# A longer-annealed instruction order for a sliding-window attention and gated convolution kernel

## The chip, the core and the metric

The kernel runs on one core of one Trainium2 chip. The metric is the device time of one execution in microseconds; a lower number is better. The core has five engines that run at the same time, each through its own list of instructions in order: TensorE (PE, with its weight loads shown apart as PEld), VectorE (DVE), ScalarE (ACT), GpSimd (POOL), and SyncE (SP), which here only issues DMA transfers. They meet at semaphores.

## The reference

Attention over 8 batches and 8 heads, 576 positions and head size 64, in which a position sees only the 32 positions on either side, followed by a feed-forward block with a three-tap convolution along the sequence and a sigmoid gate:

```python
# attention: q, k, v are (8, 8, 576, 64)
scores = scale * np.matmul(q, k.transpose(0, 1, 3, 2))
mask = np.abs(pos[:, None] - pos[None, :]) <= 32
scores = np.where(mask, scores, -1000000000.0)
attn = softmax(scores)
x = np.matmul(attn, v)            # heads put side by side: (8, 576, 512)
# feed-forward block
h = np.maximum(x @ w_in, 0.0)     # 512 -> 1024
conv_out[s] = sum(conv_w[k] * h[s + k - 1] for k in range(3))   # per channel, zeros outside
out = h * sigmoid(conv_out) @ w_out                              # 1024 -> 512
```

All inputs and the output are 32-bit floats.

## The kernel before

**The work.** The attention is done batch by batch, and each batch in two halves of 288 rows (`attention(b)`, s = 0 and 1). A half is loaded by SP into staging tiles (`load_qk`, `load_v`), cast to bf16 (`cast_qk` into qn and kn, `cast_v` and `shift_v` into ve and vo; for batches after the second these casts are POOL's alone), transposed on PE and copied to qT and kT (`transposes`), multiplied into 128 x 64 score blocks (`scores`: L669), put through the exponential on ACT (L684), multiplied with v (`values`: L712), normalised on DVE (L730, L732) and transposed into xT (`turn`: on PE for the first two batches, by a DMA transpose of SP for the others).

The feed-forward block works on 12 chunks of 384 rows, three for each pair of batches. `hidden` makes eight tiles of 128 channels for a chunk: four matmuls with w_in (L857), a relu with a factor of one half on ACT (L877) into hT, the three taps, a tanh on ACT (L955, since sigmoid(x) is half of one plus tanh(x/2)), and the gate on DVE (L972) into gT. `project` multiplies gT with w_out (L997), copies the result to y (on ACT or DVE), and SP stores y (L1015, for the last chunk L1011). Two large weight matrices are loaded through two staging tiles wst and cast (`load_w`).

**The choices.** Some operations can be done in several ways, and the number in `CHOICE` says how.

- For each group of scores, 0 adds the mask's large negative number on PE ahead of the scores (L658, with the constant tile `band`), 1 multiplies the exponentials by a 0/1 mask on POOL, 2 does so on DVE (both are L691).
- For the taps of each of the eight tiles of a chunk, the list `KINDS` says which taps are done on PE (L932, with a diagonal weight matrix), on ACT (L940), on DVE (L945) and on POOL (L920 for the product, L925 for the sum): 0 is two taps on PE and one on DVE, 1 is one on PE and two on DVE, 2 is one on ACT and two on DVE, 3 is all three on POOL (three instructions and then two more), 4 is all three on PE.

**The order.** Nothing in the kernel is scheduled by the compiler. `Plan.add` records every operation with what it reads and writes. `Plan.place` then walks through the operations as the list `ORDER` names them, takes the engine from `PICK` where an operation may run on more than one (casts, copies, diagonal weights, y), takes a PSUM bank from `BANKS` for each operation that opens a PSUM slot (there are eight banks), and gives each operation a planned start. The instructions are emitted in the order of the planned starts. So the four lists CHOICE, ORDER, PICK and BANKS decide every engine's list of instructions, and which operations share a bank. `WARM` adds matmuls that compute nothing into gaps of the first 36 planned microseconds (L1024); there are 19 of them.

**Names that the text uses.** "A tap" on ACT is L940, on DVE L945; "a mask" is L691; a "POOL pair" is the three instructions L920, L920, L925 and a "POOL single" the two L920, L925 that follow it for choice 3. tmp is the tile in which POOL gathers its taps; the tanh that follows reads it. Lines of the changed kernel are smaller by one.

```python
        if alt is not None:
            if CHOICE[alt[0]] not in alt[1]:
                return None
...
        order, banks = [self.ops[i] for i in ORDER], iter(BANKS)
        for op in order:
            e = op.eng = PICK.get(op.idx) or next(iter(op.on))
```

Of the kernel before, what the change touches and what calls it, by code (L numbers as in the profile page):

```python
# [17 lines left out]
    0, 0, 2, 0, 0, 2, 0, 2, 2, 0, 4, 4, 4, 3, 4, 4, 4, 4, 0, 4, 0, 4, 4, 4, 0, 4, 2, 2, 0, 0, 1, 4,  # L18
    0, 4, 0, 4, 0, 4, 4, 4, 0, 0, 4, 2, 4, 0, 2, 2, 2, 2, 0, 2, 2, 4, 0, 3, 2, 4, 4, 2, 2, 4, 3, 3,
    2, 2, 2, 2, 2, 0, 0, 1, 2, 2, 3, 2, 1, 1, 4, 2, 2, 2, 0, 2, 2, 2, 4, 2, 3, 0, 2, 4, 3, 2, 2, 3,  # L20
    2, 1, 2, 2, 3, 2, 2, 0, 0, 2, 2, 2, 2, 1, 4, 3, 2, 4, 3, 0, 2, 0, 2, 2, 1, 2, 0, 2, 3, 2, 3, 2,
    0, 2, 2, 3, 2, 2, 3, 2, 3, 2, 2, 2, 3, 1, 3, 2, 2, 3, 2, 0, 2, 2, 3, 3,
# [11 lines left out]
    30, 37, 0, 1, 2, 11, 9, 29, 36, 51, 47, 28, 52, 35, 27, 34, 45, 46, 49, 50, 48, 55, 56, 53, 31,  # L34
    18, 38, 41, 26, 68, 75, 32, 42, 43, 33, 44, 24, 3, 39, 60, 17, 20, 16, 61, 7, 6, 54, 57, 70, 77,
    69, 76, 91, 87, 88, 67, 74, 85, 86, 89, 58, 59, 62, 92, 63, 64, 65, 90, 22, 117, 121, 120, 4,
    98, 96, 97, 99, 66, 225, 227, 226, 15, 228, 10, 118, 112, 113, 40, 73, 93, 94, 25, 8, 213, 71,
    81, 115, 251, 214, 80, 135, 142, 217, 221, 222, 119, 242, 218, 252, 235, 223, 84, 13, 5, 243,
    114, 215, 224, 236, 14, 95, 116, 219, 220, 23, 72, 82, 253, 79, 83, 244, 237, 78, 103, 104, 105,
    134, 141, 154, 100, 150, 21, 155, 133, 140, 132, 139, 152, 148, 248, 216, 153, 101, 102, 110,  # L40
    149, 111, 106, 108, 109, 238, 151, 159, 239, 249, 107, 254, 266, 232, 268, 160, 250, 256, 267,
    290, 386, 229, 19, 255, 269, 291, 136, 174, 137, 138, 146, 257, 233, 230, 387, 234, 264, 376,
    265, 156, 377, 292, 231, 12, 293, 258, 382, 245, 262, 259, 157, 263, 383, 274, 384, 385, 260,
    261, 240, 275, 277, 380, 246, 284, 158, 180, 278, 241, 279, 381, 281, 388, 389, 247, 280, 171,
    172, 306, 143, 144, 177, 178, 147, 390, 294, 276, 285, 286, 282, 270, 295, 283, 391, 185, 186,
    164, 271, 173, 179, 191, 192, 413, 287, 272, 296, 414, 165, 166, 161, 406, 307, 312, 145, 305,
    304, 311, 162, 392, 273, 163, 393, 394, 288, 289, 187, 378, 189, 169, 416, 379, 188, 167, 409,
    170, 168, 419, 415, 410, 190, 417, 407, 408, 418, 420, 199, 200, 320, 321, 193, 122, 126, 124,
    125, 123, 395, 324, 322, 411, 402, 412, 435, 127, 323, 399, 194, 436, 403, 437, 400, 404, 401,
    325, 396, 195, 397, 421, 398, 318, 319, 422, 129, 131, 128, 130, 297, 298, 196, 326, 329, 438,  # L50
    197, 330, 308, 313, 176, 182, 175, 183, 184, 405, 439, 198, 466, 467, 331, 181, 201, 202, 204,
    203, 205, 301, 340, 341, 346, 356, 343, 342, 347, 354, 327, 440, 206, 441, 309, 316, 328, 357,
    423, 431, 358, 352, 353, 302, 355, 432, 359, 424, 427, 425, 426, 428, 310, 317, 314, 332, 333,
    334, 364, 365, 362, 363, 335, 336, 337, 315, 360, 361, 474, 473, 480, 491, 492, 433, 434, 207,
    457, 442, 449, 429, 446, 299, 461, 458, 443, 450, 462, 451, 463, 444, 459, 460, 447, 448, 430,
    208, 445, 366, 209, 211, 487, 345, 344, 475, 476, 350, 348, 511, 510, 509, 481, 454, 493, 351,
    452, 464, 210, 212, 453, 455, 494, 489, 490, 552, 553, 300, 465, 349, 367, 456, 488, 370, 371,
    372, 368, 369, 498, 499, 515, 525, 500, 526, 546, 547, 495, 496, 554, 555, 512, 516, 521, 522,
    523, 524, 660, 661, 667, 678, 497, 679, 527, 528, 548, 549, 550, 529, 674, 551, 530, 570, 562,
    571, 675, 572, 532, 534, 535, 533, 563, 573, 531, 578, 468, 469, 574, 479, 478, 486, 483, 477,  # L60
    482, 485, 504, 505, 501, 502, 506, 558, 559, 560, 567, 503, 579, 536, 561, 589, 580, 575, 576,
    577, 581, 582, 513, 519, 339, 374, 373, 568, 338, 603, 605, 601, 606, 602, 564, 484, 514, 520,
    470, 586, 565, 604, 471, 590, 569, 566, 591, 592, 587, 518, 517, 540, 541, 542, 537, 538, 588,
    593, 609, 610, 556, 617, 611, 607, 557, 583, 612, 539, 613, 633, 625, 626, 608, 627, 697, 618,
    634, 622, 614, 584, 662, 695, 698, 702, 663, 508, 375, 507, 732, 733, 635, 619, 628, 585, 623,
    624, 668, 734, 735, 709, 710, 638, 676, 736, 620, 621, 639, 636, 637, 737, 680, 792, 629, 696,
    701, 303, 793, 799, 596, 681, 643, 677, 597, 644, 645, 707, 708, 711, 712, 640, 594, 595, 646,
    738, 806, 807, 630, 631, 632, 647, 641, 642, 713, 714, 739, 615, 616, 748, 749, 598, 720, 715,
    648, 649, 810, 599, 700, 794, 795, 753, 721, 716, 717, 718, 650, 651, 750, 811, 652, 740, 741,
    722, 685, 682, 683, 800, 686, 746, 747, 757, 665, 664, 672, 704, 670, 699, 703, 706, 669, 666,  # L70
    673, 762, 744, 763, 767, 764, 765, 768, 769, 545, 544, 543, 869, 870, 770, 751, 758, 766, 745,
    754, 759, 752, 684, 472, 653, 657, 654, 771, 755, 760, 761, 808, 775, 809, 658, 655, 656, 780,
    719, 705, 889, 671, 796, 690, 812, 813, 865, 866, 742, 875, 797, 827, 828, 983, 829, 801, 833,
    881, 756, 743, 772, 867, 776, 777, 778, 691, 781, 692, 782, 723, 779, 882, 883, 876, 783, 784,
    687, 688, 724, 868, 879, 884, 773, 880, 689, 804, 873, 874, 897, 817, 725, 726, 871, 818, 774,
    885, 886, 887, 872, 982, 989, 877, 878, 1000, 902, 893, 1001, 727, 728, 888, 802, 985, 798, 805,
    822, 894, 898, 899, 895, 896, 814, 815, 785, 789, 909, 830, 984, 600, 900, 816, 890, 786, 891,
    903, 790, 823, 901, 990, 843, 844, 905, 998, 824, 910, 911, 904, 831, 835, 892, 906, 819, 820,
    999, 907, 908, 912, 787, 788, 693, 694, 729, 730, 923, 924, 996, 834, 841, 842, 921, 1002, 922,
    937, 839, 927, 928, 837, 803, 913, 821, 997, 1003, 1004, 1005, 942, 1018, 1111, 1017, 1023, 943,  # L80
    659, 1112, 1007, 1008, 951, 925, 845, 926, 840, 938, 952, 939, 953, 846, 940, 941, 954, 955,
    914, 946, 944, 945, 947, 915, 1006, 933, 934, 948, 935, 936, 1118, 850, 986, 991, 851, 852, 853,
    854, 855, 929, 931, 932, 949, 950, 961, 962, 963, 930, 956, 957, 916, 917, 847, 1129, 1029,
    1030, 958, 964, 848, 965, 1130, 918, 1125, 1126, 987, 992, 988, 994, 995, 1009, 959, 1010, 832,
    825, 826, 731, 1058, 970, 1054, 1059, 919, 993, 1011, 849, 971, 960, 966, 967, 1055, 838, 968,
    1060, 1061, 972, 1056, 1033, 836, 856, 1062, 1113, 969, 1034, 1080, 973, 1063, 1064, 857, 858,
    1057, 1012, 1085, 1065, 1070, 1081, 974, 1019, 1020, 1114, 1119, 1024, 1035, 1036, 1082, 1086,
    1083, 1075, 975, 1115, 791, 976, 1066, 1067, 1092, 1088, 1021, 1025, 1071, 1013, 1072, 1073,
    1014, 1084, 1087, 859, 860, 1076, 861, 1031, 1032, 977, 1027, 1089, 1116, 1121, 1042, 1097,
    1090, 978, 1043, 1022, 1028, 1093, 1074, 1091, 1098, 1131, 1132, 1094, 1095, 1127, 1039, 1040,  # L90
    1077, 1078, 1026, 979, 980, 1037, 1038, 1044, 1096, 1128, 1135, 1041, 1099, 1079, 1068, 1069,
    1136, 1149, 1146, 1148, 1153, 1147, 1152, 1123, 1048, 1049, 1050, 1133, 1134, 1045, 1046, 1015,
    1117, 1124, 1160, 1164, 1165, 862, 864, 863, 1193, 1194, 1162, 1195, 1196, 1183, 1184, 1137,
    1047, 1163, 1161, 1120, 1138, 1139, 1100, 1101, 1227, 1141, 1142, 1140, 920, 981, 1016, 1143,
    1222, 1223, 1185, 1186, 1191, 1199, 1102, 1103, 1192, 1218, 1204, 1200, 1187, 1158, 1159, 1188,
    1189, 1106, 1190, 1209, 1197, 1205, 1201, 1202, 1213, 1107, 1224, 1206, 1203, 1214, 1207, 1208,
    1215, 1228, 1219, 1198, 1225, 1231, 1210, 1226, 1216, 1217, 1229, 1230, 1211, 1104, 1105, 1212,
    1220, 1221, 1108, 1109, 1168, 1166, 1169, 1171, 1172, 1151, 1051, 1052, 1247, 1167, 1248, 1249,
# [1002 lines left out]
```

## Time and profile before

| What | Number |
|---|---|
| Time, median of 4 runs | 221.8 us (220.61 to 222.16) |
| The profiled execution's own time | 221.26 us |
| Its span, first to last instruction | 219.5 us |
| Instructions | 6461 |
| PE busy | 201.8 us (92%) |
| DVE busy | 194.4 us (89%), 397 instructions |
| ACT busy | 185.0 us (84%), 392 instructions |
| POOL busy | 184.8 us (84%), 233 instructions |
| Granted TensorE clock | 1.000 |
| DMA | 45.92 MB, mean 209 GB/s |

"Busy" is the time in which at least one instruction of the engine was under way. A recorded duration reaches from an instruction's start to its end, and an engine may start the next before that end, so that durations add up to more than the busy time. A matmul's end is modelled, so PE's row says less about PE than the others' rows do about them.

### The profile page before, as it was taken

The numbers are of one execution on the slowest core, as the hardware profiler recorded it, in microseconds if no ns is written. First come the engines' busy times: TensorE is split into PE (matmuls) and PEld (weight loads), VectorE is DVE, ScalarE is ACT, GpSimd is POOL, SyncE is SP. The second block draws the span as 40 slices with busy tenths as digits, with TensorE's granted clock in tenths as the row PEclk, the third lists the DMA queues.
The fourth block names the chain that finished last, engine by engine and source line by source line (L and its number), as shares of the span: only waits on it lengthen the run. The fifth ranks groups of instructions, "written<-read, shape, count | busy, mean of one in ns | idle before, by whom it ended". The sixth has DMA issues, their size and how long they took to land.

```text
span 219.5 us, 6461 instructions
## 1 busy us (share of the span) xinstructions
PE 201.8 (92%) x2462; PEld 125.7 (57%) x2462; DVE 194.4 (89%) x397; ACT 185.0 (84%) x392; POOL 184.8 (84%) x233
## 2 busy tenths in 40 slices
PE   2677889999999999999999999999999999999983
PEld 1445669865777456656466565555566465454442
DVE  5488795998899999999999999999999989999952
ACT  1358989899699978999989999989998999999750
POOL 4142899889999999999999999999999999999940
PEclk9999999999999999999999999999999999999999
DMA  5999999999998599995879999599989631130334
GB/s 160 225 344 293 272 236 278 362 248 274 270 347 163 104 275 248 290 181 179 241 223 296 115 329 205 150 313 252 178 292 132 109 146 29 32 143 3 145 125 162
DMA packets 68675, 45.92 MB, mean 209 GB/s; under 512 B 53644, under 2 KB 53924, under 8 KB 68644
## 3 DMA queue, kind: packets, MB, share of 16 engines
q1 hardware_dynamic: 68608, 45.49, 82.7%
q8 instruction: 19, 0.31, 0.6%
q14 instruction: 12, 0.10, 0.1%
q10 hardware_dynamic: 36, 0.01, 0.0%
HBM read 32.52 MB, written 9.44 MB: 191 GB/s over the span
## 4 chain that ended last, share of the span: by engine, by line
POOL 66%; DMA 10%; issue 9%; DVE 5%; ACT 3%; PE 2%; SPq 2%; POOLq 0%; DVEq 0%; ACTq 0%
POOL tmp L925 16%; POOL tmp L920 16%; POOL vo L403 14%; POOL ve L403 8%; POOL kn L403 6%; DMA wst<-in_moe_w_out_dram 5%; POOL qn L403 4%; DMA vst<-in_v_dram 4%; DMA out_dram<-y 2%; POOL attn L691 1%; SPq L506 1%; POOL w_out_sb L403 1%; ACT attn L684 1%; DVE xn L732 1%; DVE diag_w L492 1%
## 5 line engine op out<-in xcount | busy, mean ns | idle before, releaser
L857 PE MATMUL ps_all<-xT,w_in_sb 128*128 128x385 bf16 (+4 forms) x448 | 74.3, 305 | 2.1 <-ACT attn L684 0.8
L997 PE MATMUL ps_all<-w_out_sb,gT 128*128 128x512 bf16 (+1 forms) x296 | 66.8, 373 | 0.9 <-DVE gT L972 0.6
L945 DVE SCALAR_TENSOR_TENSOR ps_all<-hT,conv_w_sb,ps_all 128x384 f32<-128x384 bf16 (+2 forms) x110 | 61.9, 589 | 2.8 <-ACT hT L877 0.9
L972 DVE SCALAR_TENSOR_TENSOR gT<-ps_all,hT 128x384 bf16<-128x384 f32 (+3 forms) x112 | 52.3, 493 | 3.4 <-ACT ps_all L955 2.8
L857 PEld LDWEIGHTS <-w_in_sb 128*128 128x128 bf16 x448 | 40.3, 98 | 23.2 <-issue 1.1
L877 ACT ACTIVATE hT<-ps_all 128x385 bf16<-128x385 f32 (+4 forms) x112 | 47.8, 457 | 5.2 <-PE ps_all L857 4.6
L997 PEld LDWEIGHTS <-gT 128*128 128x128 bf16 x296 | 28.1, 98 | 30.6 <-issue 1.1
L925 POOL TENSOR_TENSOR tmp<-tmp 128x384 f32<-128x384 f32 (+1 forms) x42 | 41.7, 992 | 3.5
L684 ACT ACTIVATE attn<-ps_all 128x1024 bf16<-128x1024 f32 (+1 forms) x40 | 36.1, 942 | 5.3 <-PE ps_all L669 5.3
L955 ACT ACTIVATE ps_all<-ps_all 128x384 f32<-128x384 f32 (+3 forms) x91 | 37.9, 437 | 2.5 <-DVE ps_all L945 1.2
L920 POOL TENSOR_SCALAR tmp<-hT,conv_w_sb 128x384 f32<-128x384 bf16 (+1 forms) x63 | 37.3, 599 | 1.9
L403 POOL TENSOR_SCALAR vo<-vst 64x1024 bf16<-64x1024 f32 (+1 forms) x31 | 33.8, 1092 | 3.5 <-DMA vst<-in_v_dram 1.0
L403 POOL TENSOR_SCALAR ve<-vst 128x512 bf16<-128x512 f32 (+1 forms) x39 | 25.3, 656 | 6.6 <-DMA vst<-in_v_dram 5.1
L732 DVE TENSOR_TENSOR xn<-ps_all,rec 128x512 bf16<-128x512 f32 (+1 forms) x32 | 25.9, 819 | 0.6
L940 ACT ACTIVATE ps_all<-hT,conv_w_sb 128x384 f32<-128x384 bf16 (+1 forms) x42 | 24.4, 588 | 0.5 <-DVE gT L972 0.3
L401 ACT COPY y<-ps_all 128x512 f32<-128x512 f32 (+1 forms) x31 | 18.4, 594 | 6.1 <-PE ps_all L997 5.6
L691 DVE TENSOR_TENSOR attn<-attn,mask 128x1024 bf16<-128x1024 bf16 (+1 forms) x22 | 21.0, 961 | 1.8 <-ACT attn L684 1.7
L403 POOL TENSOR_SCALAR kn<-kst 128x1152 bf16<-128x1152 f32 (+1 forms) x18 | 18.3, 1021 | 3.8 <-DMA kst<-in_k_dram 2.9
L932 PE MATMUL ps_all<-hT,diag_w 128*128 128x384 bf16 (+3 forms) x121 | 20.0, 275 | 0.8 <-ACT hT L877 0.7
L401 ACT COPY kT<-ps_all 128x512 bf16<-128x512 bf16 (+1 forms) x22 | 16.3, 753 | 4.0 <-PE ps_all L609 3.6
L712 PEld LDWEIGHTS <-attn 128*64 128x64 bf16 x640 | 13.0, 111 | 9.4 <-issue 5.5
L712 PE MATMUL ps_all<-ve,attn 128*64 128x65 bf16 x384 | 16.2, 197 | 2.2 <-POOL ve L403 0.9
(66 smaller groups left out, 232.3 us busy)
## 6 DMA issues: line engine op xcount, KB each, us to landing
kst<-in_k_dram SPq DMA_DIRECT2D x32, 288.0 KB, 4.8
qst<-in_q_dram SPq DMA_DIRECT2D x32, 288.0 KB, 5.5
out_dram<-y SPq DMA_DIRECT2D x11, 768.0 KB, 5.8
vst<-in_v_dram SPq DMA_DIRECT2D x23, 256.0 KB, 5.5
vst<-in_v_dram SPq DMA_DIRECT2D x16, 192.0 KB, 6.3
wst<-in_moe_w_in_dram SPq DMA_DIRECT2D x2, 1024.0 KB, 9.1
wst<-in_moe_w_out_dram SPq DMA_DIRECT2D x2, 1024.0 KB, 10.8
out_dram<-y SPq DMA_DIRECT2D x2, 256.0 KB, 2.0
```

The costliest lines, as they stand in the source:

```text
L401: nc.scalar.copy(out=out_, in_=in_)
L403: nc.gpsimd.tensor_scalar(out=out_, in0=in_, scalar1=1.0, scalar2=0.0, op0=ALU.mult, op1=ALU.add)
L684: add(act(2 * w), t + 0.1, lambda e: nc.scalar.activation(at, ps(sl, 0, 1024).rearrange("p (e x) -> p e x", e=2)[:, :, 0:w], AF.Exp, bias= ...
L712: nc.tensor.matmul(ps(sl, lo, lo + D + 1, 64 * j, 64 * j + 64), attn[a][:, 512 * h_ + col:512 * h_ + col + 64], (vo if tt % 2 else ve)[i][ ...
L857: nc.tensor.matmul(ps(sl, 512 * y, 512 * y + n), w_in_sb[:, kc, m * 128:(m + 1) * 128], x_[:, kc, a0:a1], start=(kc == 0), stop=(kc == KC ...
L877: nc.scalar.activation(o_, i_, AF.Relu, bias=0.0, scale=0.5)
L920: nc.gpsimd.tensor_scalar(out=tv(not own), in0=hview(m, o0, o1, kk - 1), scalar1=conv_w_sb[:, kk, m:m + 1], scalar2=0.0, op0=ALU.mult, op1 ...
L925: nc.gpsimd.tensor_tensor(out=tv(0), in0=tv(0), in1=tv(1), op=ALU.add)
L945: add("DVE", tt + 0.1, lambda e, m=m, y=y, n_=n_, pv=pv, ks=by_dve: nc.vector.scalar_tensor_tensor(out=pv(y), in0=hview(m, o0, o1, ks[n_] ...
L955: nc.scalar.activation(o_, i_, AF.Tanh, bias=0.0, scale=1.0)
L972: nc.vector.scalar_tensor_tensor(out=o_, in0=i_, scalar=1.0, in1=hview(m0, o0, o1, 0, w), op0=ALU.add, op1=ALU.mult,)
L997: nc.tensor.matmul(ps(sl, f0, f1), gT[ig][:, m, 128 * i:128 * i + 128], w_out_sb[:, m, f0:f1], start=(m == 0), stop=(m == MB - 1),)
```

## The change

The four lists CHOICE, ORDER, PICK and BANKS are replaced by others; all functions, all costs and due times in `TIMES`, and all tiles stay. CHOICE and PICK change which engine does some operations; ORDER has 1432 operations in place of 1431. The program holds the same transfers. Counted in both built programs: masks on DVE 22 before and 16 after, masks on POOL 2 and 4, groups of scores whose mask is added on PE 16 and 20; taps on ACT 42 and 48, on DVE 110 and 117, on PE 121 and 113, tiles with their taps on POOL 21 and 19 (20 and 18 of them of full width); diagonal weights on ACT 9 and 15, on DVE 15 and 9.

```diff
 CHOICE = [
-    0, 0, 2, 0, 0, 2, 0, 2, 2, 0, 4, 4, 4, 3, 4, 4, 4, 4, 0, 4, 0, 4, 4, 4, 0, 4, 2, 2, 0, 0, 1, 4,
-    0, 4, 0, 4, 0, 4, 4, 4, 0, 0, 4, 2, 4, 0, 2, 2, 2, 2, 0, 2, 2, 4, 0, 3, 2, 4, 4, 2, 2, 4, 3, 3,
-    2, 2, 2, 2, 2, 0, 0, 1, 2, 2, 3, 2, 1, 1, 4, 2, 2, 2, 0, 2, 2, 2, 4, 2, 3, 0, 2, 4, 3, 2, 2, 3,
-    2, 1, 2, 2, 3, 2, 2, 0, 0, 2, 2, 2, 2, 1, 4, 3, 2, 4, 3, 0, 2, 0, 2, 2, 1, 2, 0, 2, 3, 2, 3, 2,
-    0, 2, 2, 3, 2, 2, 3, 2, 3, 2, 2, 2, 3, 1, 3, 2, 2, 3, 2, 0, 2, 2, 3, 3,
+    0, 0, 0, 0, 1, 0, 0, 2, 0, 0, 4, 4, 4, 4, 3, 2, 4, 4, 4, 4, 0, 4, 4, 4, 2, 4, 0, 2, 0, 0, 0, 4,
+    4, 4, 4, 4, 4, 4, 4, 4, 4, 4, 0, 4, 2, 1, 1, 2, 2, 0, 2, 0, 2, 4, 3, 4, 4, 2, 2, 2, 1, 2, 1, 2,
+    3, 0, 3, 2, 2, 2, 2, 2, 0, 2, 2, 3, 0, 1, 2, 2, 4, 0, 0, 2, 1, 2, 4, 2, 2, 2, 2, 3, 2, 3, 2, 0,
+    2, 0, 2, 2, 2, 2, 1, 1, 0, 2, 2, 3, 2, 1, 4, 2, 2, 0, 3, 2, 2, 0, 2, 0, 2, 2, 2, 2, 4, 3, 3, 2,
+    3, 3, 2, 2, 2, 2, 2, 2, 2, 2, 2, 3, 2, 2, 3, 3, 2, 2, 3, 2, 3, 2, 3, 2,
 ]
...
 ORDER = [
-    30, 37, 0, 1, 2, 11, 9, 29, 36, 51, 47, 28, 52, 35, 27, 34, 45, 46, 49, 50, 48, 55, 56, 53, 31,
...
-    1425, 1426, 1416, 1417, 1418, 1427, 1428, 1429, 1430,
+    67, 74, 0, 29, 36, 30, 27, 34, 37, 51, 1, 47, 2, 22, 12, 21, 48, 52, 28, 35, 45, 49, 50, 46, 55,
...
+    1417, 1418, 1419, 1425, 1428, 1426, 1427, 1429, 1430, 1431,
 ]
 PICK = {
-    3: "DVE", 4: "ACT", 5: "DVE", 6: "DVE", 7: "DVE", 8: "DVE", 9: "DVE", 10: "ACT", 11: "ACT",
...
+    3: "ACT", 4: "ACT", 5: "DVE", 6: "ACT", 7: "ACT", 8: "ACT", 9: "ACT", 10: "DVE", 11: "ACT",
...
 BANKS = [
-    6, 4, 6, 5, 3, 2, 0, 2, 0, 6, 5, 4, 5, 3, 6, 4, 0, 1, 2, 0, 6, 2, 4, 3, 6, 0, 1, 5, 4, 2, 6, 0,
...
+    3, 0, 2, 0, 1, 0, 2, 5, 6, 6, 4, 2, 0, 4, 6, 3, 0, 4, 6, 3, 2, 1, 0, 6, 5, 4, 2, 0, 6, 5, 4, 3,
...
```

How SP's list of transfers begins in the two programs, in the names of the reference (b is the batch, s the half, c the block of 128 rows of v):

```text
before: k b0 s0 (2), q b0 s0 (2), v c0, q b0 s1, v c1, v c2, k b0 s1 (2), q b0 s1, w_in (2), v c4, v c2, k b1 s0, v c3, k b1 s0, q b1 s0 (2),
        v b1 c0, k b1 s1, v b1 c1, v b1 c2, q b1 s1 (2), k b2 s0, k b1 s1, k b2 s0, q b2 s0 (2), w_out (2)
after:  q b0 s1, k b0 s0 (2), q b0 s0 (2), q b0 s1, v c1, v c2, k b0 s1 (2), v c0, v c3, w_in (2), v c2, v c4, q b1 s0 (2), k b1 s0 (2),
        q b1 s1 (2), v b1 c0, k b1 s1, w_out (1), k b1 s1, v b1 c1, v b1 c2, w_out (1), k b2 s0 (2), q b2 s0 (2)
```

## The prediction

> **What bounds the kernel now.** I read the busy times of the page first, then the 40 slices, the chain that ended last, the busy times of four stretches, the waits inside the longest of them, and at last POOL's own timeline.
>
> ```profile
> PE 201.8 (92%) x2462; PEld 125.7 (57%) x2462; DVE 194.4 (89%) x397; ACT 185.0 (84%) x392; POOL 184.8 (84%) x233
> ...
> POOL 4142899889999999999999999999999999999940
> ...
> POOL 66%; DMA 10%; issue 9%; DVE 5%; ACT 3%; PE 2%; SPq 2%; POOLq 0%; DVEq 0%; ACTq 0%
> ```
>
> The first line shows four engines within 10% of each other, and no clear bound. The second shows POOL full from the sixth slice on. The third says that the work that ended last goes back through POOL for two thirds of the span.
>
> ```profile
> core 0: us, PE busy (x) PEld busy (x) DVE busy (x) ACT busy (x) POOL busy (x), PEclk, DMA share, GB/s
> 0.00:48.50 48.50, 37.24 (x562) 28.76 (x563) 37.01 (x104) 34.60 (x85) 30.60 (x52) 1.00 1.03 268
> 48.50:63.00 14.50, 14.00 (x256) 9.85 (x255) 12.51 (x25) 12.01 (x24) 13.92 (x14) 1.00 1.04 295
> 63.00:211.50 148.50, 146.51 (x1624) 85.01 (x1622) 143.25 (x269) 136.94 (x283) 140.26 (x169) 1.00 0.77 182
> 211.50:219.50 8.00, 4.08 (x25) 2.07 (x22) 1.67 (x3) 1.41 (x3) 0.00 (x0) 0.99 0.52 197
> ```
>
> The cuts are chosen: at 48.5 the first projection of chunk 0 begins, at 63.0 the last one of chunk 0 has been issued, at 211.4 POOL's last tap ends. The head is short of data: no compute engine is full before 48.5, and the DMA engines are (share 1.03). From 63.0 to 211.5 DVE is idle for 148.5 - 143.25 = 5.3 us, ACT for 11.6, and POOL, by this row, for 8.2. The timeline says what POOL's 8.2 are:
>
> ```profile
> 184.86 1.00 POOL L925 TENSOR_TENSOR tmp<-tmp 128x384 f32<-128x384 f32 x1
> 185.84 1.15 POOL L920 TENSOR_SCALAR tmp<-hT,conv_w_sb 128x384 f32<-128x384 bf16 x2
> 187.07 1.00 POOL L925 TENSOR_TENSOR tmp<-tmp 128x384 f32<-128x384 f32 x1
> 188.16 0.58 POOL L920 TENSOR_SCALAR tmp<-hT,conv_w_sb 128x384 f32<-128x384 bf16 x1
> ```
>
> From 187.07 + 1.00 = 188.07 to 188.16 POOL waits for nothing; a gap of up to 0.1 us stands between its instructions everywhere (8.2 us over 169 instructions is 49 ns each), and the list of POOL's waits after the w_out cast at 46 us is empty. So POOL is in truth occupied all the time from 46 to 211.4. Who waits for it in that stretch:
>
> ```profile
> ACT hT L877 <- PE ps_all L857: 4.0, 11, 0.8
> ...
> ACT ps_all L955 <- POOL tmp L925: 3.2, 7, 0.8
> DVE gT L972 <- ACT ps_all L955: 1.7, 6, 0.4
> ...
> DVE rec L730 <- PE ps_all L712: 1.1, 4, 0.4
> ...
> PE ps_all L712 <- POOL vo L403: 0.4, 1, 0.4
> PE ps_all L712 <- POOL ve L403: 0.4, 1, 0.4
> ```
>
> Only 3.2 + 0.4 + 0.4 = 4.0 us of waits name POOL, but each stands in a queue that is nearly full, and the tail starts from POOL: its last tap ends at 211.42, the tanh follows at 211.46, the gate at 211.98, then 20 matmuls (3.67 us), a copy (0.37) and the last store (2.0). The chain shows a wait for the store of chunk 10 near the end; I don't believe it, since DVE's copy at 214.77 coincides with the tenth of those matmuls, whose result it copies.
>
> **The change part by part.** Prices are mean times from the start of one instruction to the start of the engine's next (a pause counted up to 0.1 us), worked out from the trace of before: recorded durations overlap and would count too much (397 DVE instructions last 219 us in sum and keep DVE busy for 194). ACT: tap 0.54, tap of 192 columns 0.36, copy of 640 columns 0.68, of 512 0.61, y 0.55, diagonal 0.34, cast 0.55. DVE: tap 0.55, of 192 0.33, gate of 192 0.29, copy 0.77 and 0.65, y 0.68, mask 0.97 (half width 0.78), diagonal 0.35. POOL: tiles of choice 3 need a pair (2.33) and a single (1.70); mask 2.21, q or k cast 1.18, ve cast 0.67. I count operations in both programs before and after the last projection of chunk 0.
>
> Head, to that point. ACT: 6 diagonals +2.0, 2 ve casts +1.1, 2 copies -1.4, 2 y -1.1, one cast less -0.7, taps, tanhs and turns of part width +1.5: +1.4. DVE: 4 masks -3.9, 6 diagonals -2.1, 2 y +1.4, small ones +0.7: -3.9. POOL: one wide cast +1.2, two ve -1.3, a k and a vo cast +1.5, a w_in cast -0.7: +0.7. Nothing of this moves the head in my sum: ACT is idle there for 48.5 - 34.6 = 13.9 us, DVE for 11.5, POOL for 17.9. Without that cover, ACT's +1.4 would be the price.
>
> Transfers of the head. One half of q that is needed later now stands ahead of the first k in SP's queue: one issue, 0.6 us, for the first cast (before at 4.19, after a wait of 1.43 for kst) and all behind it, and v block 3 ahead of w_in. On the other side w_out is asked for earlier. Before, 12.0 MB had been issued up to and with it and it landed at 45.9 us, 262 GB/s. After, 9.0 MB stand up to its first half and 10.8 up to its second, so at that rate 34 and 41 us, an estimate: 4.6 earlier. But PE is busy for 19.04 of the 20 us from 40 to 60, so not more than about 1 us can be had from projecting earlier. Bounds -1.0 and +0.6; I take 0, since the two ends are near each other.
>
> Stretch after it (148.5 us before). ACT: 6 taps +3.2, a half tap +0.4, copies of q and k +2.9 (six wide ones more, two narrow ones fewer), one y, three tanhs and relus of part width and a turn -1.7: +4.8. DVE: 8 taps +4.4, 6 wide copies -4.6, 3 narrow ones +2.0, masks (three half, less one whole) -1.4, y +0.7, part-width taps and gates -0.9: +0.2. POOL: two pairs -4.7, two singles -3.4, two masks +4.4, a q or k cast -1.2, a ve cast +0.7: -4.2, the gaps between instructions being in the prices. PE: 8 fewer diagonal matmuls and 8 more with `band` come to about 640 columns fewer of some 470,000; I count 0.
>
> So POOL's queue could end 4.2 us earlier. It can't all be had. DVE's floor in the stretch is its work, 143.25 + 0.2, and the waits that have nothing to do with POOL (1.7 + 1.1): 146.2, so at most 148.5 - 146.2 = 2.3 us. ACT's is 136.94 + 4.8 and the waits for PE's relu input (4.0): 145.7, at most 2.8 us. The smaller, 2.3, is the gain of the stretch.
>
> Tail. Both end with 20 matmuls, copy and store after the last gate. Before, that gate is tile 6, straight after POOL's last tap. After, tile 7, with an ACT tap and two DVE taps, is queued behind tile 6: one more tap (0.55) and one more gate (0.50) on DVE, of which the tap lies beside the tanh: +0.5. The y copies of the last chunk no longer go to ACT first; they wait for the same matmuls and cost nothing new. The store of chunk 7 moves to just ahead of that of chunk 9, and the first y copy of chunk 9 waits for it; both have 768 KB and land in 3.4 to 6.7 us. Before, DMA is at 0.22 of its share from 191 to 210, so it lands in time; without that, up to 6.7 us for ACT's queue, which I leave to the range.
>
> Sum: 0 - 2.3 + 0.5 = -1.8 us. The profiled execution took 221.26 us (span 219.5 and 1.8 around it), 0.5 below the median of the runs; so 219.5 for it, and from the median 221.8 - 1.8 = 220.0.
>
> Two rules speak against this. The Trainium skill, Perfetto Trace Analysis, section "Identifying the Most-Contended Engine", says to take the engine with the highest occupancy as the bottleneck, and not to trust matmul busy time. By the rows that is DVE (143.25 of 148.5), whose work in the stretch grows by 0.2: the rule makes the sum 0 + 0.2 + 0.5 = +0.7. I follow the timeline, in which POOL's gaps aren't free, but the rule is what keeps me from taking all of 4.2. The other row, with shortest, median and longest duration in ns, is
>
> ```profile
> L691 DVE TENSOR_TENSOR attn<-attn,mask x22: 420/916/1519, 24.4 to 178.4; 128x1024 bf16<-128x1024 bf16 x17, 128x512 bf16<-128x512 bf16 x5
> ```
>
> with a spread no other DVE group has. SBUF — State Buffer, section "Who interferes with whom", says that a DVE instruction with two SBUF inputs and a GpSimd instruction that reads SBUF exclude each other for a whole instruction. Six fewer such DVE masks ease that (at 0.3 over the median each, 1.8 us at most), but four POOL masks of 2.1 us in place of two hold DVE's masks longer, up to 2.1 us for each of two more. By the rule alone -1.8 to +4.2; by the row, in whose mean price the collisions are, what stands in the sum.
>
> **The rivals.** First, POOL is the bound and gives back time: 220.0, with the head between -1.0 and +0.6. For it: POOL's unbroken queue. Chance 0.45.
>
> Second, DVE is the bound and always was: between 221.8 and 222.5, by the occupancy sum. For it: 5.3 us idle in 148.5. Against: of those, waits for tanhs that themselves waited for POOL. Chance 0.22.
>
> Third, slower: ACT becomes the bound. It gets 4.8 us more in the stretch, 141.7 of 148.5, and keeps 6.8 us for waits. It waits 11.6 us now, of which 3.2 name POOL and go. If all of the other 8.4 remain, the stretch needs 150.1, +1.6, and with the tail's +0.5 the time is 223.9. It decides once more than 6.8 of the 8.4 us of waits remain (the tail apart). For it: taps and wide copies are put on ACT in every third of the stretch, and what is queued behind a late ACT tap is a relu, then PE's slot. If not even the POOL waits go, +4.8 and +0.5: 227.1. Chance 0.33.
>
> That the change doesn't do what it says is excluded by the counts in the programs: the order is different on every engine.
>
> **How the numbers follow.** About 0.5%, 1.1 us, is what a measurement of this kernel can tell from no change. The first case lies at 220.0, under 220.7, the second within the band, the third above 222.9: faster 0.45, same 0.22, slower 0.33. The range runs from 217.4 (all of POOL's 4.2 us and a head 1.0 earlier, less the tail's 0.5, is -4.7 or 217.1, of which I leave out a little) to 225.0 (the third case at 223.9 and a part of the way to its worst end). The first case's own range is 218.5 to 220.7.
>
> **What would show it.** Right: the stretch from the last projection of chunk 0 to POOL's last tap shorter than 148.5 by about 2, POOL with real waits in it, ACT's waits for tmp below 3.2, DVE idle there under 4. Second case: POOL waits, the stretch as before. Third: ACT busy over 143 of the stretch, and PE, DVE and POOL waiting for it more than now. A head that ends later than 63.6 would mean that the early q costs more than I took. A chain that still runs through POOL for two thirds at a shorter time would show that its work was the measure; one through ACT, that the third case holds. Wrong altogether: PE or SP as the engine that the chain runs through.

## The result, and the profile after

The changed kernel takes 220.3 us (median of 29 runs) against 221.85 us (48 runs of the kernel before): a ratio of 0.9928, 95% interval 0.9912 to 0.9944, or 1.55 us less. The forecast was 220.0. Since the first profile of the changed kernel came from an execution at the top of its range (222.13 us), all lines "after" are from a second profile of the same program, called a_again below: execution 220.11 us, span 218.4 us (before: 221.26 and 219.5).

The page of a_again: busy times by engine, POOL's row of the 40 slices, and the chain that ended last, by engine.

```profile
PE 201.0 (92%) x2462; PEld 125.7 (58%) x2462; DVE 193.0 (88%) x391; ACT 189.2 (87%) x406; POOL 180.2 (83%) x225
...
POOL 3351999999896967899999999999999999999940
...
PE 40%; POOL 28%; DVE 17%; DMA 4%; issue 4%; ACT 4%; SPq 1%; POOLq 1%; DVEq 0%
```

In the whole run POOL has 4.6 us less to do (184.8 before), ACT 4.2 us more, DVE 1.4 us less. POOL's row has holes now, from the 11th to the 17th slice (55 to 93 us, down to 6 tenths), and its share of the chain has fallen from 66% to 28%. A reader who stopped here would say that POOL was the bound before and that PE is now. The experiments bear out the first of these and do not settle the second. The shares of the chain are no firm reading either: in a_dve_less, an experiment below whose time is the same, POOL has 44% of it and PE 26%.

The same four stretches as before, a_again:

```profile
core 0: us, PE busy (x) PEld busy (x) DVE busy (x) ACT busy (x) POOL busy (x), PEclk, DMA share, GB/s
0.00:48.50 48.50, 37.89 (x560) 29.09 (x560) 34.00 (x91) 36.39 (x91) 33.16 (x55) 1.00 1.02 286
48.50:63.00 14.50, 13.83 (x265) 10.54 (x263) 12.64 (x25) 11.03 (x25) 13.44 (x15) 1.00 1.04 261
63.00:211.50 148.50, 146.06 (x1624) 84.20 (x1621) 144.05 (x273) 141.40 (x291) 133.63 (x157) 1.00 0.76 180
211.50:220.00 8.50, 3.18 (x21) 1.87 (x20) 2.27 (x4) 0.37 (x1) 0.00 (x0) 0.95 0.45 169
```

The clock is 1.00 in both kernels but for the last matmuls, so the difference between these two executions is not a matter of the clock. In the long stretch ACT is busy for 141.40 of 148.5 us, against 136.94 before, and yet the run is faster. POOL is busy for 133.63 against 140.26.

The waits in that stretch, a_again (total us, times, longest one):

```profile
POOL tmp L919 <- ACT hT L876: 2.7, 2, 2.1
...
POOL vo L402 <- DMA vst<-in_v_dram: 2.0, 1, 2.0
...
POOL kn L402 <- DMA kst<-in_k_dram: 1.5, 1, 1.5
DVE gT L971 <- ACT ps_all L954: 1.4, 3, 0.9
...
ACT ps_all L954 <- POOL tmp L924: 1.1, 3, 0.8
```

POOL, which waited for nothing before, now waits 6.2 us in these three rows, for a relu and for two loads. ACT's waits for POOL's tmp have fallen from 3.2 to 1.1 us.

With the landmarks of the prediction in place of fixed cuts (the last projection of chunk 0 as DVE's queue passes it, and the end of POOL's last tap), the span splits as follows.

| | Before | After | Difference | Forecast |
|---|---|---|---|---|
| Head, to the last projection of chunk 0 | 63.0 | 64.4 | +1.4 | 0 |
| Stretch, to POOL's last tap | 148.4 | 146.0 | -2.4 | -2.3 |
| Tail, to the last instruction | 8.1 | 8.0 | -0.1 | +0.5 |
| Span | 219.5 | 218.4 | -1.1 | -1.8 |

By ACT's queue the head is 0.8 us later instead of 1.4, and by PE's own start of that projection 0.9 (62.84 and 63.72 us). The medians differ by 1.55 us where these two executions differ by 1.1, so each row of the table carries the chance of two single executions. Some of the experiments below leave the head as it is, and their traces show the spread: DVE's queue passes the landmark at 62.95, 62.97 and 63.19 us in three executions with the head of before, and at 63.48, 64.05 and 64.38 in three with the changed head. Their medians lie 1.1 us apart (0.5 by PE's start).

### The profile page after: what moved, and what is told of

Same layout as the page of the kernel before. It is cut to its first block, busy times and chain, and to the rows that moved or that the text cites. A ratio compares the mean times of both kernels' runs of the same rounds, so it can differ in the third digit from the quotient of the medians.

```text
span 220.4 us, 6459 instructions
## 1 busy us (share of the span) xinstructions
PE 200.6 (91%) x2462; PEld 125.2 (57%) x2462; DVE 193.1 (88%) x391; ACT 189.2 (86%) x406; POOL 180.2 (82%) x225
## 4 chain that ended last, share of the span: by engine, by line
POOL 52%; PE 16%; DVE 12%; issue 6%; DMA 6%; ACT 3%; SPq 3%; POOLq 1%; DVEq 0%
POOL tmp L924 14%; POOL tmp L919 13%; POOL vo L402 9%; POOL ve L402 6%; DMA kst<-in_k_dram 6%; PE ps_all L996 5%; POOL kn L402 4%; POOL qn L402 4%; POOL attn L690 3%; PE ps_all L608 3%; PE ps_all L856 3%; PE ps_all L931 2%; SPq L505 2%; DVE xn L731 2%; DVE w_in_sb L406 1%
## 5 line engine op out<-in xcount | busy, mean ns | idle before, releaser
L944 DVE SCALAR_TENSOR_TENSOR ps_all<-hT,conv_w_sb,ps_all 128x384 f32<-128x384 bf16 (+3 forms) x117 | 65.7, 595 | 3.7 <-PE ps_all L931 2.0
L876 ACT ACTIVATE hT<-ps_all 128x385 bf16<-128x385 f32 (+4 forms) x112 | 48.4, 466 | 4.7 <-PE ps_all L856 4.5
L924 POOL TENSOR_TENSOR tmp<-tmp 128x384 f32<-128x384 f32 (+1 forms) x38 | 37.6, 991 | 3.2
L683 ACT ACTIVATE attn<-ps_all 128x1024 bf16<-128x1024 f32 (+1 forms) x40 | 37.1, 952 | 2.6 <-PE ps_all L668 2.4
L919 POOL TENSOR_SCALAR tmp<-hT,conv_w_sb 128x384 f32<-128x384 bf16 (+1 forms) x57 | 33.9, 603 | 2.8 <-ACT hT L876 1.2
L939 ACT ACTIVATE ps_all<-hT,conv_w_sb 128x384 f32<-128x384 bf16 (+3 forms) x49 | 28.3, 584 | 2.5 <-DVE gT L971 1.8
L402 POOL TENSOR_SCALAR qn<-qst 128x1152 bf16<-128x1152 f32 (+1 forms) x19 | 19.2, 1017 | 7.4 <-DMA qst<-in_q_dram 6.3
L400 ACT COPY y<-ps_all 128x512 f32<-128x512 f32 (+1 forms) x28 | 16.4, 594 | 5.3 <-PE ps_all L996 5.3
L608 PE MATMUL ps_all<-ident,kn 128*128 128x128 bf16 x144 | 13.1, 224 | 7.6 <-DVE kn L406 6.1
L400 ACT COPY kT<-ps_all 128x640 bf16<-128x640 bf16 (+1 forms) x21 | 15.8, 758 | 2.5 <-PE ps_all L608 1.5
L931 PE MATMUL ps_all<-hT,diag_w 128*128 128x192 bf16 (+3 forms) x113 | 17.1, 271 | 0.0
```

What stands on the lines that cost most here:

```text
L400: nc.scalar.copy(out=out_, in_=in_)
L402: nc.gpsimd.tensor_scalar(out=out_, in0=in_, scalar1=1.0, scalar2=0.0, op0=ALU.mult, op1=ALU.add)
L683: add(act(2 * w), t + 0.1, lambda e: nc.scalar.activation(at, ps(sl, 0, 1024).rearrange("p (e x) -> p e x", e=2)[:, :, 0:w], AF.Exp, bias= ...
L876: nc.scalar.activation(o_, i_, AF.Relu, bias=0.0, scale=0.5)
L919: nc.gpsimd.tensor_scalar(out=tv(not own), in0=hview(m, o0, o1, kk - 1), scalar1=conv_w_sb[:, kk, m:m + 1], scalar2=0.0, op0=ALU.mult, op1 ...
L924: nc.gpsimd.tensor_tensor(out=tv(0), in0=tv(0), in1=tv(1), op=ALU.add)
```

## The experiments

**The same 5 us taken from each engine in turn, in the kernel before.** If an engine's work is the measure, taking some of it away shortens the run; if not, nothing happens. Each of these four kernels skips some instructions of one engine, nearly all of them in the long stretch, so its output is incomplete. The sizes given are counted, at the mean time from one start to the next. The busy times of the pages fall by other amounts: POOL's by 5.9 us, DVE's by 2.6, ACT's by 3.6 and PE's by 1.9.

POOL, the single of three tiles (5.1 us):

```diff
+                NPT[0] += bool(by_pool)
+                cut = bool(by_pool) and NPT[0] in (5, 9, 13)
...
+                        if cut and not begin:
+                            return
```

> The kernel before, with the third tap (two POOL instructions, 1.70 us) left out in three of the tiles whose taps are on POOL, one each in chunks 4, 6 and 8: 5.1 us less POOL work, nothing else moved. If POOL's queue is the bound (my theory): 2 to 3 us less time, to DVE's floor. If DVE is the bound: under 0.5 us. If all four engines share the bound: about 1 us, as for each of the other three.

Measured: 220.04 us against 221.80; ratio 0.9915, interval 0.9882 to 0.9948. So 5.1 us less work on POOL buys 1.8 us (by the interval 1.2 to 2.6), a price of 1.8 / 5.1 = 0.35 us of time for each us of work, a little under the 2 to 3 us expected. Where the rest went is in the waits of that kernel in the long stretch:

```profile
POOL tmp L925 <- ACT hT L878: 3.0, 3, 2.4
...
ACT ps_all L960 <- POOL tmp L930: 1.8, 3, 0.8
POOL kn L403 <- DMA kst<-in_k_dram: 1.7, 1, 1.7
```

A relieved POOL catches up with its own inputs: 3.0 us of waiting for relus and 1.7 for a load of k, none of which were there before. Most of what POOL was spared became waiting. The cut also shortens the work on each of the three tiles by 1.7 us, which could be a gain of its own; the next cut shortens nine tiles by 0.55 us each and gains nothing.

DVE, the second tap of nine tiles (5.0 us):

```diff
+                cut = len(by_dve) == 2 and NDT[0] in (8, 11, 14, 18, 22, 26, 30, 35, 40)
...
-lambda e, ...: nc.vector.scalar_tensor_tensor(
+lambda e, ..., cut=cut: cut and n_ == 1 or nc.vector.scalar_tensor_tensor(
```

> The kernel before, with the second DVE tap left out in nine tiles of chunks 3 to 9: 5.0 us less DVE work. POOL is the bound: under 0.5 us less. DVE is the bound: 2.5 to 5 us less. A shared bound: about 1 us less.

Measured: 221.71 us; 0.9999, interval 0.9966 to 1.0033. The engine with the most work on record in the stretch, after PE, shows no price: by the interval at most 0.8 us for this cut. Its row of the long stretch:

```profile
63.00:211.50 148.50, 146.40 (x1624) 84.93 (x1622) 140.27 (x260) 136.86 (x282) 140.09 (x169) 1.00 0.73 182
```

DVE is down by 3.0 us to 140.27, and POOL stands at 140.09 as before (140.26). DVE only got more idle time, and POOL did not move.

ACT, half of eleven exponentials (4.8 us), and PE, one of the eight matmuls of 23 projections (5.0 us):

```diff
+        v = w // 2 if u is not None and NEX[0] in (10, 12, 14, ..., 30) else w
-        at = attn[a].rearrange("p (e x) -> p e x", e=2)[:, :, 0:w]
+        at = attn[a].rearrange("p (e x) -> p e x", e=2)[:, :, 0:v]
```

```diff
-                    for m in range(m0, m1):
+                    for m in range(m0, m1 - cut):
```

> The kernel before, with the second half of the exponential left out in 11 groups of scores of the batches after the second: 4.8 us less ACT work. POOL or DVE is the bound: under 0.5 us less. A shared bound: about 1 us less. ACT has 11.6 us idle in the stretch, so a gain near the whole 4.8 would speak against both of my theories.

> The kernel before, with the last of the eight matmuls left out in 23 projections of chunks 1 to 10: 23 x 0.216 = 5.0 us less PE work. POOL or DVE is the bound: under 0.5 us less. If PE, whose busy time the page can't judge, is the bound: 3 to 5 us less. A shared bound: about 1 us less.

Measured: 221.97 us for ACT (0.9984, 0.9948 to 1.002) and 222.12 us for PE (0.9995, 0.9964 to 1.0026). Neither shows a price: by the intervals at most 1.2 us for ACT and 0.8 for PE. Of the four engines POOL alone shows one in the kernel before. The test of PE is the weakest, as its busy time fell by only 1.9 us.

**The same in the changed kernel, for POOL, DVE and ACT.** The singles cut are those of POOL's 5th, 8th and 11th tile, and the other cuts are moved in the same way; a_again is the changed kernel itself, run beside them (its ratio agrees with that of all runs, 0.9928, within the intervals).

```diff
-                cut = bool(by_pool) and NPT[0] in (5, 9, 13)
+                cut = bool(by_pool) and NPT[0] in (5, 8, 11)
...
-                cut = len(by_dve) == 2 and NDT[0] in (8, 11, 14, 18, 22, 26, 30, 35, 40)
+                cut = len(by_dve) == 2 and NDT[0] in (10, 15, 18, 21, 26, 31, 35, 40, 46)
```

> The changed kernel once more, for an undisturbed profile and as the base of the next three runs: 220.3 us, 1.6 us under the kernel before. If POOL was the bound before and its 4.2 us of work less is what paid, POOL shows real waits in the stretch from 63 us on, and the waits of ACT for tmp are below 3.2 us. If the gain came from the head, the stretch is as long as before (148.5 us).

> The changed kernel with the third tap left out in three of its tiles on POOL, in chunks 4, 7 and 8: 5.1 us less POOL work. If POOL is still the bound: another 1.5 to 2 us under the changed kernel, as in the same cut of the kernel before (1.8). If the bound has passed to ACT or DVE: under 0.5 us.

> The changed kernel with the second DVE tap left out in nine tiles of chunks 3 to 10: 5.0 us less DVE work. If DVE's floor ended the gain, as the prediction has it: 1 us or more under the changed kernel. If POOL is still the bound: no difference, as in the kernel before.

> The changed kernel with the second half of the exponential left out in 11 groups of scores: 4.8 us less ACT work, which is what the change added to ACT in the stretch. If ACT has become the bound (the third case): 1 us or more under the changed kernel. If not: no difference.

| Kernel | Median, us | Ratio to before | Interval |
|---|---|---|---|
| a_again | 220.44 | 0.9957 | 0.9935 to 0.9979 |
| a_pool_less | 217.63 | 0.9828 | 0.9797 to 0.9859 |
| a_dve_less | 220.37 | 0.9945 | 0.9921 to 0.9969 |
| a_act_less | 220.66 | 0.9947 | 0.9921 to 0.9972 |

DVE and ACT still show no price: their intervals lie over that of a_again. POOL's is 220.44 - 217.63 = 2.8 us for 5.1 us of work, 0.55 for each us, more than the 1.5 to 2 us expected. Against the ratio of all 29 runs (0.9928) the same cut is worth 2.2 us, 0.43 for each us; with intervals this wide, a rise over the 0.35 of before is not shown. So POOL's work still bears on the time of the changed kernel, and DVE's and ACT's don't, though POOL waits for 6.2 us in its stretch and its share of the chain is 28%. Chain and row of the long stretch in a_pool_less:

```profile
PE 62%; DVE 28%; ACT 3%; issue 2%; DMA 2%; SPq 1%; DVEq 0%; ACTq 0%
```

```profile
63.00:211.50 148.50, 147.51 (x1638) 85.58 (x1636) 143.76 (x273) 140.82 (x291) 129.46 (x151) 1.00 0.79 186
```

Here POOL is gone from the chain, and PE is busy for 147.51 of 148.5 us. That hints at PE as the next bound, and no more than hints: PE stood at 146.51 in the kernel before, where a cut of its work gained nothing. No run took PE's work away in the changed kernel, so PE's price there stays open.

**The four masks of POOL given to another engine.** A mask costs POOL about 2.1 us (the half one 1.15), 7.7 us in all. a_masks_dve gives the four to DVE and a_masks_pe adds them on PE; both compute everything.

```diff
-CHOICE[4], CHOICE[84], CHOICE[102], CHOICE[103] = 1, 1, 1, 1
+CHOICE[4], CHOICE[84], CHOICE[102], CHOICE[103] = 2, 2, 2, 2    # a_masks_dve
+CHOICE[4], CHOICE[84], CHOICE[102], CHOICE[103] = 0, 0, 0, 0    # a_masks_pe
```

> The changed kernel with its four POOL masks done on DVE at the same places of the order: POOL 7.9 us less (three at 2.21, one at 1.24), DVE 3.7 us more (three at 0.97, one at 0.78); the result is computed in full. POOL is the bound at the price measured in the cut of its taps (2.8 us of time for 5.1 us of work) and DVE is free: 4 us under the changed kernel, about 216. DVE's floor counts: 0 to 2 us slower than that. If POOL's masks sit where POOL has slack: no difference.

> The changed kernel with the same four masks added on PE ahead of the scores (eight more matmuls with band, some 1.5 us of PE time at most): POOL 7.9 us less and DVE unchanged; computed in full. POOL is the bound: as the version with the masks on DVE, about 216. If that one is slower than this one, the difference is what DVE's work and its collisions with POOL cost. If PE is close behind POOL: 1 us slower than the version on DVE.

Measured: a_masks_dve 220.66 us against 221.79 (0.9945, 0.9914 to 0.9977), no gain over the change; a_masks_pe 219.17 us (0.9871, 0.9828 to 0.9914), the fastest of the complete kernels, about 1.2 us under the changed kernel. By POOL's mean price of 0.55, 7.7 us would be worth 4.2, as both expectations had it. They are not, and POOL's own timeline shows where they lie: first a_again (start, duration, line, operation),

```profile
132.44 2.12 POOL L690 TENSOR_TENSOR attn<-attn,mask 128x1024 bf16<-128x1024 bf16 x1
134.53 2.27 POOL L402 TENSOR_SCALAR qn<-qst 128x1152 bf16<-128x1152 f32 x2
136.76 4.39 POOL L690 TENSOR_TENSOR attn<-attn,mask 128x1024 bf16<-128x1024 bf16 x2
141.24 2.67 POOL L402 TENSOR_SCALAR vo<-vst 64x1024 bf16<-64x1024 f32 x2
```

and then a_masks_dve (the bracket is the idle time before it and what ended it):

```profile
134.90 1.15 POOL L398 TENSOR_SCALAR qn<-qst 128x1152 bf16<-128x1152 f32 x1 [2.09 <-DMA qst<-in_q_dram]
140.07 2.16 POOL L398 TENSOR_SCALAR vo<-vst 64x1024 bf16<-64x1024 f32 x2 [4.02 <-DMA vst<-in_v_dram]
```

Three masks stood exactly where POOL is ahead of its loads: without them the casts of v come only 141.24 - 140.07 = 1.2 us earlier, at the moment that v lands, and 2.09 + 4.02 us of the 6.5 turn into waits. The window from 126 to 160 us, in a_again, a_masks_dve and a_masks_pe in turn, says who does the masks instead:

```profile
126.00:160.00 34.00, 33.17 (x438) 19.88 (x436) 33.79 (x62) 32.48 (x65) 32.66 (x33) 1.00 0.84 226
```

```profile
126.00:160.00 34.00, 32.77 (x436) 19.86 (x433) 33.82 (x64) 32.79 (x64) 25.55 (x29) 1.00 0.86 221
```

```profile
126.00:160.00 34.00, 33.79 (x467) 20.73 (x470) 33.30 (x63) 33.54 (x65) 26.41 (x30) 1.00 0.85 225
```

POOL is far from full in the last two (25.55 and 26.41 of 34). DVE is already at 33.79 in a_again, so in a_masks_dve, at 33.82, three more masks find little room; in a_masks_pe DVE has 0.7 us left, and PE takes the masks. The end of the k-th of the 37 y copies shows the course (all from the profiled executions, us):

```
            3rd    12th   18th   27th   33rd   36th
before      56.6   110.7  145.0  193.0  211.4  215.9
a_again     61.5   114.9  145.8  192.0  210.2  214.8
masks_dve   59.8   113.7  143.8  191.5  209.7  214.3
masks_pe    60.6   114.4  145.0  190.8  209.0  213.6
pool_less   60.9   114.6  144.3  189.6  207.2  212.0   (in the changed kernel)
wout_early  60.7   114.7  148.9  197.0  215.3  219.9   (in the kernel before)
```

Single executions of kernels with the same head differ by up to 0.9 us at the 3rd copy (60.6 in a_dve_less, 61.5 in a_again), so small leads say nothing. a_masks_dve is ahead of a_again by 1.7 us at first (the mask at 22 us, before which POOL waited 2.7 us for the exponential, is gone from its queue), by 2.0 at the 18th copy, and by only 0.5 at the 27th. From the 18th to the 27th it takes 47.7 us, a_again 46.2 and a_masks_pe 45.8: it loses its lead in and after the window where DVE is full. That the full DVE is the reason is read from these rows; no run tests it apart. a_masks_pe is ahead by 0.8 at the 18th and by 1.2 at the end.

The masks also show what one engine's work does to another's. DVE's masks by shape, a_again and then a_masks_pe (busy us, mean ns of one):

```profile
L690 DVE TENSOR_TENSOR attn<-attn,mask 128x1024 bf16<-128x1024 bf16 x14 | 13.8, 1001 | 0.0
L690 DVE TENSOR_TENSOR attn<-attn,mask 128x512 bf16<-128x512 bf16 x2 | 2.6, 1280 | 0.0
```

```profile
L587 DVE TENSOR_TENSOR attn<-attn,mask 128x1024 bf16<-128x1024 bf16 x14 | 12.5, 910 | 0.0
L587 DVE TENSOR_TENSOR attn<-attn,mask 128x512 bf16<-128x512 bf16 x2 | 1.4, 702 | 0.0
```

The same sixteen masks take 16.4 us on DVE while POOL does four of its own, and 13.9 us when POOL does none. But only one of the sixteen meets a mask on POOL, one of half width. In a_again, and then in a_masks_pe:

```profile
137.03 2.14 DVE L690 TENSOR_TENSOR attn<-attn,mask 128x512 bf16<-128x512 bf16 x1
```

```profile
137.33 0.41 DVE L587 TENSOR_TENSOR attn<-attn,mask 128x512 bf16<-128x512 bf16 x1
```

In a_again POOL is at two masks of its own from 136.76 on, as its timeline above shows, and DVE's mask lasts 2.14 us; in a_masks_pe POOL does nothing at that time, and the mask lasts 0.41 us. That is 1.7 of the 2.5 us. The rest is a balance of masks that fall beside other work of POOL in one kernel and not in the other: the mask at 157.70 us in a_again takes 1.63 us beside a cast of q, the same mask 0.68 us in a_masks_pe, where POOL is idle. No run shows that the 2.5 us cost time; DVE shows no price above.

**Two moves in SP's queue.** The change asks for w_out earlier, and puts one half of q ahead of the first k. b_wout_early does the first alone in the kernel before, and a_q_back takes the second out of the changed kernel (two warm-up matmuls on PE fall elsewhere with it).

```diff
-... 306, ..., 173, ..., 304, 122, ..., 127, ...    # ORDER, before: 122 and 127 load w_out
+... 122, 306, ..., 173, 127, ..., 304, ...         # b_wout_early
```

```diff
-67, 74, 0, 29, 36, ..., 68, 75, ...    # ORDER, after: 67 loads half of q, 74 casts it
+0, 29, 36, ..., 67, 74, 68, 75, ...    # a_q_back
```

> The kernel before, with the two loads of w_out moved ahead in SP's queue to where the changed kernel has them; every other engine's list is the same. POOL waits 1.8 us for w_out in the kernel before. If POOL is the bound already in the head: up to 1.8 us less. If the head is bound by the transfers, whose sum stays: no difference, or up to 1 us more for the q and k halves that now come later.

> The changed kernel, with the half of q that leads SP's queue put back behind the four loads that the first scores need, and its DVE cast with it. I took 0.6 us as the most that the early q costs: 0 to 0.6 us under the changed kernel. If the planned head relies on it: slower.

Measured: b_wout_early 225.22 us (1.0133, 1.0082 to 1.0184), 3.4 us slower than before by the medians and more than anything expected. a_q_back 220.09 us (0.992, 0.988 to 0.996), no different from the changed kernel.

POOL's timeline around the casts of w_out, first in the kernel before:

```profile
42.93 2.37 POOL L403 TENSOR_SCALAR w_out_sb<-wst 128x512 bf16<-128x512 f32 x4 [1.04 <-DMA wst<-in_moe_w_out_dram]
46.06 2.36 POOL L403 TENSOR_SCALAR w_out_sb<-wst 128x512 bf16<-128x512 f32 x4 [0.76 <-DMA wst<-in_moe_w_out_dram]
```

then in b_wout_early:

```profile
39.83 0.67 POOL L325 TENSOR_SCALAR kn<-kst 128x576 bf16<-128x576 f32 x1 [2.44 <-DMA kst<-in_k_dram]
43.80 1.15 POOL L325 TENSOR_SCALAR kn<-kst 128x1152 bf16<-128x1152 f32 x1 [3.29 <-PE ps_all L854]
...
47.37 5.12 POOL L325 TENSOR_SCALAR w_out_sb<-wst 128x512 bf16<-128x512 f32 x8
```

The weights went ahead of k in SP's queue, so k landed later, and in POOL's queue the casts of k still stand ahead of those of w_out: POOL waits 2.44 us for k and then 3.29 us for PE, and casts w_out at 47.37 instead of 42.93 and 46.06. The last of these casts ends at 52.49 instead of 48.42, 4.1 us later. The table above shows what becomes of it: 4.1 us late at the 3rd copy, 4.0 at the 36th. What is late there is passed to the end nearly one to one. PE had little to do for a while, and then the granted clock fell, which the row of b_wout_early shows (0.88; it was 1.00 before):

```profile
48.50:63.00 14.50, 12.21 (x167) 7.78 (x168) 9.82 (x19) 9.64 (x20) 14.01 (x17) 0.88 0.75 203
```

From 50 to 52 us PE was busy for 0.79 us; then the clock was 0.53 and 0.62 in the next two stretches of 2 us. The 4.1 us are there when POOL's last cast of w_out ends, just as the low clock begins; what the clock adds later, no run separates.

a_q_back starts its first relu at 23.1 us; six executions with the early q start it at 23.3 to 24.2, five in the kernel before and its cut versions at 21.7 to 22.7. Its 3rd y copy ends at 60.6 us and its last projection of chunk 0 starts at 63.48, both within what a_dve_less (60.6, 62.83) and a_again (61.5, 63.72) show with the early q. So the early q costs the first relu up to 1 us by these executions, and no cost at the end of the head is shown.

## Why the prediction was right, point by point

**What bounds the kernel.** Right, and by the step that carried it: the timeline, in which POOL's gaps of up to 0.1 us are not idle time. Only POOL's work shows a price in the kernel before. The Trainium skill, Perfetto Trace Analysis, section "Identifying the Most-Contended Engine", would take the engine with the highest occupancy; by that rule DVE (143.25 of 148.5 us) stood ahead of POOL (140.26). The measurements disagree with it here: 0.9999 for DVE's 5 us, 0.9915 for POOL's. The second case falls with b_dve_less. That less work on POOL is what made the changed kernel faster rests on this price: 4.2 us at 0.35 are 1.5, and 1.55 was measured. No run gives the changed kernel back POOL's old share alone, so other parts of the new order may have had their part.

**The head.** Taken as 0, measured +0.8 to +1.4 us in the table and +0.5 to +1.1 by the medians of three executions each: about at the upper bound of 0.6, or over it. This is the step that was mis-sized. Its sign (a head that ends after 63.6) came, but the meaning given to it, a costlier early q, is not borne out: a_q_back ends its head no earlier than other executions do. The estimate for w_out held as far as it went: in a_again POOL's last cast of it ends at 43.2 instead of 48.4 us, 5.2 earlier where 4.6 was forecast, and the first projection starts 2.0 us earlier (46.33 and 48.32). Yet the last projection of chunk 0 starts later. Where the head loses that time stays open. b_wout_early shows only that the same move costs 3.4 us in the old order of the other queues.

**The stretch.** Forecast -2.3, measured -2.4 by its landmarks. The size held and half of the reason did not. POOL's busy time fell by 4.6 us in the whole run, where the count had 4.2 - 0.7 = 3.5, and only part of it came back as time, as forecast. But what kept back the rest was not "DVE's floor", 146.2 us: a_pool_less, with DVE's work unchanged, runs from the same landmark (64.05) to POOL's last tap (206.77) in 142.7 us, and a_dve_less gains nothing. In its place POOL shows waits for its own inputs, relus and loads. At the measured prices, 0.35 to 0.55, 4.2 us are worth 1.5 to 2.3 us, without any floor. So the exact 2.3 was luck.

**ACT.** The third case, which needed it to be the bound, is refuted: a_act_less gives 0.9947 beside a_again's 0.9957. Its work was counted too high: the head's +1.4 and the stretch's +4.8 make 6.2, and its busy time rose by 4.2 in the whole run. In the row from 63.0 to 211.5 it is idle for 148.5 - 141.40 = 7.1 us, of which 1.1 name POOL, so at most 6.0 of the 8.4 us of other waits remained, under the 6.8 at which the case would have decided. Waits for PE's relu input alone went from 4.0 to 1.1 us.

**The tail.** Forecast +0.5, measured -0.1. The kernel before, and then a_again:

```profile
211.98 0.56 DVE L972 SCALAR_TENSOR_TENSOR gT<-ps_all,hT 128x384 bf16<-128x384 f32 x1 [0.61 <-ACT ps_all L955]
212.60 3.67 PE L997 MATMUL ps_all<-w_out_sb,gT 128*128 128x512 bf16 x20 [0.61 <-DVE gT L972]
```

```profile
210.94 1.02 DVE L971 SCALAR_TENSOR_TENSOR gT<-ps_all,hT 128x384 bf16<-128x384 f32 x2 [0.86 <-ACT ps_all L954]
```

The second gate comes after that of tile 6, as forecast, and DVE ends 1.58 us after POOL's last tap instead of 1.12. But PE starts its last 20 matmuls 1.18 us after that tap in both (212.60 - 211.42, and 211.56 - 210.38): the gate of tile 7 ends 0.4 us later, beside the first of them, and tile 7's taps on DVE were done at 210.1, before POOL's last tap. The sum forgot this overlap.

**The sum.** That 220.0 came so near to the measured 220.3 is luck in part. The head lost time that was not forecast, the tail did not lose the 0.5 that was, and the two errors partly cancel: +1.4, -2.4 and -0.1 make -1.1 in the two executions, the medians say -1.55, and -1.8 was forecast.

**Collisions on SBUF.** The Trainium skill, SBUF — State Buffer, section "Who interferes with whom", has a DVE instruction with two SBUF inputs and a GpSimd instruction that reads SBUF shut each other out, which is borne out in kind: the DVE mask that met POOL's masks lasted 2139 ns instead of 415, about the length of one POOL mask (2124 ns at the median). In size the forecast's bounds were wide: one DVE mask met a POOL mask, not two more, and masks of 1624 ns occur with no mask on POOL. The median stayed (916 before, 924 after).

**The signs named in advance.** POOL with real waits, ACT's waits for tmp under 3.2 us (1.1), ACT under 143 us: all came. So did DVE's idle time under 4 us, between the landmarks (146.0 - 142.25 = 3.75). The chain was a poor sign. "Two thirds through POOL at a shorter time" was to show POOL's work as the measure; the chain shows 28%, and POOL's work was the measure nevertheless. PE as the engine of the chain was to show the prediction "wrong altogether", and a_again's chain has PE at 40%; the cuts of POOL's work contradict that sign.

## What to carry to other kernels

With four engines over 80% busy, neither occupancy nor the chain's shares named the bound here; cutting the same few microseconds of counted work from each engine in turn did. Price work by its place as well as its engine: what is taken off the bounding engine just ahead of a load that is not there yet only turns into a wait, and what is given to another engine must fall where that one has room. A transfer moved forward in a queue moves everything between backward, and an engine that works in order passes on the lateness of the first thing it waits for. And a landmark of one execution is one draw: look at it in every trace that has the same part unchanged.

## What the runs showed of the hardware

- An engine can have 6.2 us of waits in a stretch and its work still have a price: POOL in the changed kernel, at 0.43 to 0.55 us of time for each us of its work.
- A mask of half width on DVE took 2.14 us (a_again) while POOL was at masks of its own, and 0.41 us (a_masks_pe) with POOL idle.
- Moving the two loads of w_out forward in the DMA queue cost more than 5 us of any engine's work was worth: +3.4 us (b_wout_early).
- After 2 us in which PE was busy for 0.79, the granted clock was 0.53 and 0.62 for the next 4 us (b_wout_early, 50 to 56 us).
